# Talking-heads attention and a Fourier mixing layer on one core: two halves of a softmax step parted, memory laid out anew, and a join between two phases reordered

## The chip, the core and the metric

The kernel runs on one core of one Trainium2 chip. The metric is the time of the whole kernel in device microseconds (us). Three runs before the change took 2463.07, 2463.15 and 2467.11 us; the median is 2463.15 us. The profiled run took 2461.87 us and its recorded span is 2460.1 us, at a mean granted TensorE clock of 0.989 of full speed.

The engines are named as the profile names them: PE (matrix products), PEld (loading of weights into PE), DVE (vector engine), ACT (scalar engine), POOL (GpSimd) and SP (the engine that here only issues transfers). [...]

## What is computed

The batch is 8, there are 12 heads, 448 positions and 64 values per head. All is float32; the layer's weights arrive as float64 and are converted on the chip.

```python
# attention, "talking heads": heads are mixed before and after the softmax
scores = scale * np.matmul(q, k.transpose(0, 1, 3, 2))      # (8, 12, 448, 448)
scores = np.einsum('bhij,hg->bgij', scores, w_pre)          # first mixing
scores = scores - np.max(scores, axis=-1, keepdims=True)
attn = np.exp(scores)
attn = attn / (np.sum(attn, axis=-1, keepdims=True) + 1e-09)
attn = np.einsum('bhij,hg->bgij', attn, w_post)             # second mixing
x = np.matmul(attn, v)          # then (8, 12, 448, 64) -> (8, 448, 768)
# Fourier mixing and a feed-forward layer
mixed = np.real(np.fft.fft(np.fft.fft(x, axis=1), axis=2))
u = x + mixed
un = (u - mean(u)) / np.sqrt(var(u) + 1e-06)                # by row
out = u + np.maximum(un @ w_ch1, 0.0) @ w_ch2               # 768 -> 3072 -> 768
```

## The kernel before

There are two phases. The first (attention and Fourier transform) goes in 192 steps; a step takes ten rows of scores of all twelve heads through both mixings and the softmax. The second (feed-forward) takes 42 pairs of blocks of matrix products; it is a Strassen-like scheme with seven products in place of eight.

The order of the engines' work in a step is fixed by hand. Step `s` holds the first mixing of step `s + 2` (LM is 2), the second mixing of step `s`, and pieces of other work (`take`) that are dealt out over the steps: scores (QK), the product with v (AV), and "full" pieces, which are transposes of q, k and X and the Fourier products.

```python
    with tc.manual_schedule(engines={ET.PE, ET.DVE, ET.Activation, ET.Pool}):
        while s <= TOT - GS + AT_X[-1]:
            old = len(later)
            n = take("none", s)                 # loads
            if 0 <= s + LM < TOT:
                emit_premix(s + LM)             # PE: first mixing
            flush()
            if 0 <= s < TOT:
                emit_postmix(s)                 # PE: second mixing
            if 0 <= s + LM < TOT:
                emit_max(s + LM)                # DVE: two maxima
                emit_exp(s + LM)                # ACT: two exponentials
            take("AV", s)
            if 0 <= s < TOT:
                emit_turn(s)                    # DVE: transpose of the second mixing
            if s >= 4:
                wts.deal(1)                     # DVE: one operation on the weights
            take("QK", s)
            ...                                 # SP: gather for step s + 4
            if 0 <= s + LM < TOT:
                emit_scale(s + LM)              # DVE: reciprocal; POOL: scaling
            ...
            for _ in range(min(len(folds), 1 if n and s > 3 else 2)):
                folds.pop(0)()                  # POOL: sums for the Fourier transform
            take("full", s)
            s += 1
        flush()
        while folds:
            folds.pop(0)()
        wts.deal(1000)
```

The first mixing and its softmax. `mx` is one tile of two PSUM banks (512 float32 each), and its pool holds one of them; `nmx` is one tile for both halves. The four products of the first mixing use four quarters of the PE array (64 rows by 64 columns each).

```python
    pmx = pool("pmx", space=bass.MemoryType.PSUM)          # one buffer
    ...
    def emit_premix(T):
        mx = pmx.tile([P, 2, 512], F32, name="mx", tag="mx")
        Kr = steps[T]["Kr"]
        for x in range(2):
            for z in range(2):
                nc.tensor.matmul(mx[64 * z:64 * z + 64, x, :S],
                                 kw1[64 * x:64 * x + KR, :],
                                 Kr[64 * x:64 * x + KR, z, :], start=True, stop=True)

    def emit_max(T):
        nmx = psm.tile([P, 2], F32, name="nmx", tag="nmx")
        for x in range(2):
            nc.vector.tensor_reduce(nmx[:, x:x + 1], steps[T]["mx"][:, x, :S],
                                    axis=AX.X, op=ALU.max, negate=True)

    def emit_exp(T):
        ...
        for x in range(2):
            nc.scalar.activation(PP[:, x, :], steps[T]["mx"][:, x, :S], ACTF.Exp,
                                 bias=steps[T]["nmx"][:, x:x + 1],
                                 accum_out=den[:, x:x + 1])
```

Waits are set by tile: an instruction that reads a tile waits for all that was written to it, and the next user of a buffer waits until all readers of the last one are done. The gather of a step's scores (`Kr<-Sb`) is four transfers from SP. The tables of the Fourier transform are loaded by POOL in step 3, though they are first used in step 38 (`AT_Z`):

```python
    def emit_tables():
        for t, n in ((rows, "at"), (ts, "ts"), (tcs, "tc")):
            for p, m in _split(0, t.shape[0]):
                nc.gpsimd.dma_start(out=t[p:p + m], in_=cn[n].ap()[p:p + m])
    ...
    due("none", 3, emit_tables)
```

The join of the phases. The second phase needs the mean and the variance of the first 512 rows (`stats`), a power of the variance on POOL (`power`), the normalised rows from ACT (`norm`), their transposes (`turn`) and sums of them (`total`). Its pools are opened after those of the first phase are closed, so they lie on the same memory, and their first use waits for the last use of what lay there.

```python
    for t in range(2):
        load_u(t)
    for i in ORDER:
        load_w1(0, i)
    with tc.manual_schedule(engines={mybir.EngineType.PE, mybir.EngineType.DVE}):
        for x in range(NT2):
            stats(0, x)          # DVE
        power(0)                 # POOL, four small operations
        for x in range(NT2):
            norm(0, x)           # ACT
            turn(0, x)           # PE, ACT
        for n in range(4):
            total(0, n)          # DVE
        ...
        for n in range(NC * NTB):
            ...
            second(n, first(n))
```

## Time and profile before

| what | value |
|---|---|
| median of three runs | 2463.15 us |
| span of the profiled run | 2460.1 us |
| PE busy | 2373.4 us (96%) |
| DVE busy | 1518.6 us (62%) |
| ACT busy | 787.0 us (32%) |
| POOL busy | 779.9 us (32%) |
| moved by DMA | 372.09 MB, 151 GB/s on average |

Busy time is the union of an engine's recorded instructions. Matrix products are pipelined and their ends are modelled, so a busy PE can hide a short wait between two of them. A row of the profile's fifth part, or of a timeline, gives line, engine, operation, the tiles (`out<-in`), the shape and the count. In square brackets, or after the bar, stands how long the engine was idle before it, and what ended that idle time. L470 is the first mixing, L478 the maximum, L486 the exponential, L507 the second mixing, L444 the scores, L534 the product with v, L941 and L997 the products of the second phase. The profile cuts the span into 40 slices:

```
PE   6999999999999969999999999999999999999999
DVE  3678778788877636776566455654575467533333
ACT  3666666666666533232011011111101101111110
POOL 3577877768775541121111001100110011000000
PEclk8999999999999989999999999999999999999999
```

A slice is 61.5 us. The first phase fills slices 1 to 14, and the 6 at place 15 is the join.

### The profile page before, as it was taken

The numbers are of one execution on the slowest core, as the hardware profiler recorded it, in microseconds if no ns is written. First come the engines' busy times: TensorE is split into PE (matmuls) and PEld (weight loads), VectorE is DVE, ScalarE is ACT, GpSimd is POOL, SyncE is SP. The second block draws the span as 40 slices with busy tenths as digits, with TensorE's granted clock in tenths as the row PEclk, the third lists the DMA queues.
The fourth block names the chain that finished last, engine by engine and source line by source line (L and its number), as shares of the span: only waits on it lengthen the run. The fifth ranks groups of instructions, "written<-read, shape, count | busy, mean of one in ns | idle before, by whom it ended". The sixth has DMA issues, their size and how long they took to land.

```text
span 2460.1 us, 48351 instructions
## 1 busy us (share of the span) xinstructions
PE 2373.4 (96%) x18608; PEld 1536.8 (62%) x18608; DVE 1518.6 (62%) x3103; ACT 787.0 (32%) x2059; POOL 779.9 (32%) x1292
## 2 busy tenths in 40 slices
PE   6999999999999969999999999999999999999999
PEld 2344454444444457777777777777777777777776
DVE  3678778788877636776566455654575467533333
ACT  3666666666666533232011011111101101111110
POOL 3577877768775541121111001100110011000000
PEclk8999999999999989999999999999999999999999
DMA  5554555546554464635545354436444545343331
GB/s 137 163 168 157 173 167 170 178 150 192 169 167 141 148 220 139 190 119 203 178 144 159 102 190 135 148 102 197 131 141 130 184 123 157 120 155 118 120 116 52
DMA packets 168579, 372.09 MB, mean 151 GB/s; under 512 B 36734, under 2 KB 90006, under 8 KB 168350
## 3 DMA queue, kind: packets, MB, share of 16 engines
q1 hardware_dynamic: 129038, 260.22, 32.4%
q0 software_dynamic: 33744, 107.40, 15.0%
q8 instruction: 148, 2.42, 0.4%
q10 hardware_dynamic: 5568, 1.38, 0.3%
q14 instruction: 81, 0.66, 0.1%
HBM read 211.98 MB, written 74.34 MB: 116 GB/s over the span
## 4 chain that ended last, share of the span: by engine, by line
PE 84%; DVE 5%; ACT 4%; DMA 3%; POOL 2%; issue 1%; SPq 1%; ACTq 0%; POOLq 0%; DVEq 0%
PE psP L941 18%; PE psP L997 18%; PE psR L941 9%; PE psR L997 9%; PE mx L470 6%; PE ms L534 5%; PE psQ L997 4%; PE psQ L941 4%; PE po L507 4%; ACT PP L486 3%; PE ms L444 3%; DVE nmx L478 3%; DMA Kr<-Sb 2%; PE ms L648 2%; PE ms L632 1%
## 5 line engine op out<-in xcount | busy, mean ns | idle before, releaser
L941 PE MATMUL psP<-ub,w1t 128*128 128x256 f32 x2016 | 463.9, 380 | 0.0
L997 PE MATMUL psP<-w2t,h 128*128 128x384 f32 x1344 | 460.9, 486 | 0.0
L941 PEld LDWEIGHTS psP<-ub,w1t 128*128 128x128 f32 x2016 | 384.0, 191 | 61.1
L207 POOL DMA_DIRECT2D raw<-in_moe_w_ch_dram x120 | 68.8, 574 | 918.6 <-DVE tmp L251 905.6
L997 PEld LDWEIGHTS psP<-w2t,h 128*128 128x128 f32 x1344 | 254.4, 190 | 165.9
L486 ACT ACTIVATE PP<-mx,nmx 128x448 f32<-128x448 f32 x384 | 239.9, 629 | 275.5 <-DVE nmx L478 258.3
L497 POOL TENSOR_SCALAR PP<-PP,rcp 128x448 f32<-128x448 f32 x384 | 241.2, 637 | 261.7 <-DVE rcp L495 208.7
L478 DVE TENSOR_REDUCE nmx<-mx 128x1 f32<-128x448 f32 x384 | 221.2, 618 | 127.1 <-PE mx L470 116.9
L1003 DVE TENSOR_TENSOR u<-u,psP 128x384 f32<-128x384 f32 x336 | 183.3, 552 | 141.5 <-PE psP L997 139.3
L946 ACT COPY h<-psP 128x512 f32<-128x512 f32 x42 | 24.6, 585 | 765.7 <-PE psP L941 745.7
L470 PE MATMUL mx<-Kr,kw 60*64 60x448 f32 x1536 | 204.3, 560 | 43.5 <-ACT PP L486 33.8
L941 PE MATMUL psR<-ub,w1t 128*128 128x256 f32 x1008 | 231.3, 379 | 0.0
L997 PE MATMUL psR<-w2t,h 128*128 128x384 f32 x672 | 230.5, 486 | 0.0
L952 DVE TENSOR_TENSOR h<-h,psQ 128x512 f32<-128x512 f32 x42 | 28.9, 687 | 302.1 <-PE psQ L941 302.1
L518 DVE STREAM_TRANSPOSE Pv<-po 128x896 f32<-128x896 f32 x192 | 212.3, 1106 | 2.9 <-PE po L507 2.6
L941 PEld LDWEIGHTS psR<-ub,w1t 128*128 128x128 f32 x1008 | 191.4, 190 | 25.9
L507 PE MATMUL po<-PP,kw 60*32 60x448 f32 x3072 | 190.0, 552 | 0.8 <-DVE Pv L518 0.8
L444 PE MATMUL ms<-kT,qT 64*60 64x448 f32 (+1 forms) x1536 | 188.3, 555 | 0.0
L324 ACT COPY Sb<-ms 124x448 f32<-124x448 f32 x384 | 184.7, 541 | 8.1 <-DMA Kr<-Sb 3.8
L534 PEld LDWEIGHTS ms<-Pv,vv 64*64 64x64 f32 x5376 | 141.9, 132 | 71.0 <-issue 30.9
L997 PEld LDWEIGHTS psR<-w2t,h 128*128 128x128 f32 x672 | 127.2, 190 | 87.5
L534 PE MATMUL ms<-Pv,vv 64*64 64x120 f32 x5376 | 164.3, 267 | 2.1 <-issue 2.1
(92 smaller groups left out, 2738.4 us busy)
## 6 DMA issues: line engine op xcount, KB each, us to landing
ub<-ub SPq DMA_DIRECT2D x294, 384.0 KB
Kr<-Sb SPq DMA_DIRECT2D x768, 105.0 KB
raw<-in_moe_w_ch_dram POOLq DMA_DIRECT2D x72, 256.0 KB, 3.4
raw<-in_moe_w_ch_dram POOLq DMA_DIRECT2D x48, 384.0 KB, 3.8
w<-wst POOLq DMA_DIRECT2D x126, 128.0 KB, 3.1
w<-wst POOLq DMA_DIRECT2D x84, 192.0 KB, 3.2
w1t<-w SPq DMA_DIRECT2D x42, 384.0 KB
w2t<-w SPq DMA_DIRECT2D x42, 384.0 KB
```

What stands on the lines that cost most here:

```text
L324: (nc.scalar.copy if eng == "a" else nc.vector.tensor_copy)(out=out, in_=in_)
L444: nc.tensor.matmul(pss[x][64 * y:64 * y + r0 + 64 - lo, :S], st["qT", xx][64 * x:64 * x + 64, y, lo:r0 + 64], st["kT", xx][64 * x:64 * x + ...
L470: nc.tensor.matmul(mx[64 * z:64 * z + 64, x, :S], kw1[64 * x:64 * x + KR, :], Kr[64 * x:64 * x + KR, z, :], start=True, stop=True)
L478: nc.vector.tensor_reduce(nmx[:, x:x + 1], steps[T]["mx"][:, x, :S], axis=AX.X, op=ALU.max, negate=True)
L486: nc.scalar.activation(PP[:, x, :], steps[T]["mx"][:, x, :S], ACTF.Exp, bias=steps[T]["nmx"][:, x:x + 1], accum_out=den[:, x:x + 1])
L497: nc.gpsimd.tensor_scalar(PP[:, x, :], PP[:, x, :], rcp[:, x:x + 1], 1.0, op0=ALU.mult, op1=ALU.mult)
L507: nc.tensor.matmul(po[o:o + 32, z, :S], kw2[64 * z:64 * z + KR, y, :], PP[64 * z:64 * z + KR, :, c * HS:(c + 1) * HS], start=True, stop=True)
L518: nc.vector.transpose(g["Pv"][:, T % GT, :].rearrange("p (z s) -> p z s", z=2), steps[T]["po"][:, :, :S])
L534: nc.tensor.matmul(pss[y][64 * x:64 * x + 64, :nu * R], st["v", pr][64 * y:64 * y + 64, x, jb * D:(jb + 1) * D], _ap(Pv, 64 * y * rp + 32 ...
L941: nc.tensor.matmul(p[:, m, :], w1[i][:, kc, m * P:(m + 1) * P], ub[:, kc, :], start=i in OPENS and m == kc == 0, stop=kc == NK - 1, skip_g ...
L997: nc.tensor.matmul(p, lhs[i][:, kf, x * P:(x + 1) * P], w2[i][:, kf, :], start=i in OPENS and kf == 0, stop=kf == FM - 1, skip_group_check ...
L1003: nc.vector.tensor_tensor(us_, us_, p, op=ALU.add)
```

## The change

Four things are changed.

1. The first mixing's PSUM tile becomes two tiles of one bank, and the maxima become two tiles of one column. Thus the exponential of the first half depends only on the first half's maximum, and the next step's first half of the mixing only on the first half's exponential. Instructions and their order on each engine stay.
2. The pools of both phases are ordered by when their content is last used, so that the second phase's first tiles lie on memory that is free early.
3. The last folds (sums on POOL that the Fourier transform of the last batch needs) are taken out of the end of the first phase and stand behind the power of the first rows, which POOL's fixed order now includes.
4. The tables are loaded in four parts, in steps 9, 16, 17 and 19.

```diff
     psb = pool("psb", 2)
     pkr = pool("pkr", 3)
-    pvv = pool("pvv")
     ppp = pool("ppp", 3)
     psm = pool("psm", 4)
+    cst = pool("cst")
+    wts.open(ctx, tc)
+    pvv = pool("pvv")
     ppv = pool("ppv", 2)
 ...
-    wts.open(ctx, tc)
-    cst = pool("cst")
 ...
-    def emit_tables():
-        for t, n in ((rows, "at"), (ts, "ts"), (tcs, "tc")):
-            for p, m in _split(0, t.shape[0]):
-                nc.gpsimd.dma_start(out=t[p:p + m], in_=cn[n].ap()[p:p + m])
+    def emit_table(t, n, p0, p1):
+        for p, m in _split(p0, p1 - p0):
+            nc.gpsimd.dma_start(out=t[p:p + m], in_=cn[n].ap()[p:p + m])
 ...
     def emit_premix(T):
-        mx = pmx.tile([P, 2, 512], F32, name="mx", tag="mx")
+        mx = [pmx.tile([P, 512], F32, name="mx", tag=f"mx{x}") for x in range(2)]
         for x in range(2):
             for z in range(2):
-                nc.tensor.matmul(mx[64 * z:64 * z + 64, x, :S],
+                nc.tensor.matmul(mx[x][64 * z:64 * z + 64, :S],
 ...
     def emit_max(T):
-        nmx = psm.tile([P, 2], F32, name="nmx", tag="nmx")
+        nmx = [psm.tile([P, 1], F32, name="nmx", tag=f"nmx{x}") for x in range(2)]
         for x in range(2):
-            nc.vector.tensor_reduce(nmx[:, x:x + 1], steps[T]["mx"][:, x, :S],
+            nc.vector.tensor_reduce(nmx[x][:, :], steps[T]["mx"][x][:, :S],
 ...
-            nc.scalar.activation(PP[:, x, :], steps[T]["mx"][:, x, :S], ACTF.Exp,
-                                 bias=steps[T]["nmx"][:, x:x + 1],
+            nc.scalar.activation(PP[:, x, :], steps[T]["mx"][x][:, :S], ACTF.Exp,
+                                 bias=steps[T]["nmx"][x][:, :],
 ...
-    due("none", 3, emit_tables)
+    for at, t in ((9, (rows, "at", 0, PN)), (16, (ts, "ts", 0, PN)),
+                  (17, (tcs, "tc", 0, CW // 2)), (19, (tcs, "tc", CW // 2, CW))):
+        due("none", at, lambda t=t: emit_table(*t))
 ...
         flush()
+        wts.deal(1000)
+
+    def fold_rest():
         while folds:
             folds.pop(0)()
-        wts.deal(1000)
 ...
 # second phase
+    pst = pool("pst", 4)
+    pun = pool("pun", 2)
     pu = [pool("pu")]
+    pub = pool("pub", 11)
     pw1 = pool("pw1", 7)
-    pub = pool("pub", 11)
-    pun = pool("pun", 2)
     pw2 = pool("pw2", 7)
     ph = pool("ph")
-    pst = pool("pst", 4)
 ...
-    with tc.manual_schedule(engines={mybir.EngineType.PE, mybir.EngineType.DVE}):
+    ET = mybir.EngineType
+    with tc.manual_schedule(engines={ET.PE, ET.DVE, ET.Pool}):
         for x in range(NT2):
             stats(0, x)
         power(0)
+        fold_rest()
+    with tc.manual_schedule(engines={ET.PE, ET.DVE}):
         for x in range(NT2):
             norm(0, x)
```

In the program that results, the order of PE's, DVE's and ACT's instructions in the steps is unchanged. At the join it moves: the statistics of the first 512 rows stand among DVE's last work of the first phase; on POOL the power stands ahead of the last group's twelve sums; on ACT the first two `norm` stand ahead of the first phase's last copies (sixteen of XT, four of X), and on PE three transposes of the second phase stand after the second of the six transposes of the second-last X.

## The prediction

> **What bounds the kernel now.** I read the busy shares by window first, then the waits, then two timelines and the chain of waits. The first view cuts the span at the first mixing's first and last step (31.20 and 859.95 us) and at the first product of the second phase (903.14 us). Columns: window, its length, each engine's busy us (instructions), granted clock, DMA share, GB/s.

> ```profile
> 31.20:859.95 828.75, 786.24 (x11994) 368.57 (x11995) 637.36 (x1254) 539.04 (x1627) 581.35 (x932) 0.99 0.53 165
> 859.95:903.14 43.19, 22.69 (x437) 17.07 (x437) 13.28 (x29) 14.73 (x45) 27.65 (x42) 0.76 0.71 236
> 903.14:2460.10 1556.96, 1549.89 (x6097) 1142.18 (x6096) 861.09 (x1802) 223.42 (x372) 165.50 (x299) 1.00 0.45 142
> ```

> The second phase, 1557 us, has PE busy 99.5% and the diff leaves it alone. What can be won lies ahead of it: PE idles 828.75 - 786.24 = 42.5 us in the steps and 43.19 - 22.69 = 20.5 us at the join, 63 us in all, or 2.6% of the whole. A gain over 2% (49 us) would need nearly all of it.

> The steps come in two kinds. In the timeline of an early one the engines hand over to each other, and no two of them overlap:

> ```profile
> 47.63 0.98 PE L470 MATMUL mx<-Kr,kw 60*64 60x448 f32 x8 [0.96 <-ACT PP L486]
> 48.76 1.16 DVE L478 TENSOR_REDUCE nmx<-mx 128x1 f32<-128x448 f32 x2 [0.78 <-PE mx L470]
> 50.03 0.63 ACT L486 ACTIVATE PP<-mx,nmx 128x448 f32<-128x448 f32 x1 [1.60 <-DVE nmx L478]
> 50.66 0.62 ACT L486 ACTIVATE PP<-mx,nmx 128x448 f32<-128x448 f32 x1
> 51.43 0.98 PE L470 MATMUL mx<-Kr,kw 60*64 60x448 f32 x8 [0.99 <-ACT PP L486]
> ```

> From one first mixing to the next: 1.13 to the maxima, 1.16 for both, 0.11, 0.63 for one exponential, 0.77 from the second's start to the release. That is 3.80 us, and PE has only three groups of 0.91 (first mixing, second mixing, scores), 2.73 us, in it. In a later step the product with v is there too, and PE has no gap (here 417.71 is a v product, then scores, then the next first mixing):

> ```profile
> 416.80 0.98 PE L507 MATMUL po<-PP,kw 60*32 60x448 f32 x16
> 417.71 1.71 PE L534 MATMUL ms<-Pv,vv 64*64 64x120 f32 x56
> 419.20 0.97 PE L444 MATMUL ms<-kT,qT 64*64 64x448 f32 x8
> 419.95 0.97 PE L470 MATMUL mx<-Kr,kw 60*64 60x448 f32 x8
> ```

> Start to start that is 0.91 + 0.91 + 1.49 + 0.75 = 4.06 us. So PE sets a step with a v product, and the chain of mixing, maximum and exponential sets a lean one.

> The chain of waits shows the tables' collision, and the join:

> ```profile
> 66.06 10.96 DMA Kr<-Sb
> ...
> 890.20 3.79 POOL xf L609 x4
> 893.99 1.02 POOL mv L893
> 895.01 0.07 issue
> 895.08 0.20 POOL mv L894
> ...
> 895.65 1.03 ACT un L903
> ```

> A gather of step 8's scores is issued at 66.06 and lands at 77.02, just after the tables were issued (57.67 to 60.9). At the join the power (mv) comes behind 3.79 us of sums on POOL, though its input was ready at 884.5, and ACT and PE wait for it, PE for 16.9 us.

> [...] Here twelve products took 4.14 us after the idle stretch (903.14) and 2.75 us at 911.02.

> **Part 1, the halves.** Nothing is added or removed; waits get finer. The first exponential can start one maximum earlier (0.54), and the next first half of the mixing waits for the first exponential only. A half's own loop becomes 1.13 + 0.62 + 0.11 + 0.77 = 2.63 us in place of 3.80. So a lean step falls to what comes next: PE's 2.73 plus some lost overlap, as the halves of the mixing start 0.63 apart instead of together, or DVE's queue: 1.16 maxima, 1.10 transpose, 0.37 reciprocal, about 0.4 for a weights operation, 3.05. I take 3.15.

> I sorted the 191 step intervals by what PE has between two first mixings, and set each against the PE spacing of its pieces (0.91, 0.91, scores 0.90, v 1.45, six transposes 0.85, seven 0.98, z pair 1.56, second Fourier product 1.26):
> - scores only, 19 steps, median 3.81 against 2.72. Of these, four hold other waits (first step, tables, gathers). The other 15 average 3.9: 15 x 0.75 = 11, and the four give 2.
> - scores and six transposes, 17 steps, 8.4 us over PE's spacing in all: the chain's 0.2 each, and a few where DVE came late. Those also get the chain's new 1.17 us of slack. I take 5.
> - scores and v, 82 steps, median 4.09 against 4.09; 13.5 over in all, but 6.6 of it are gathers in steps 8 and 24. Of the 6.9 left, half: 3.5.
> - the rest, 16 us over in all; many at PE's wall: 5.

> Sum 26.5. Some will run into DVE, or into gathers that are wanted sooner; I keep three quarters: 20 us.

> **Part 2, tables.** Steps 7, 8 and 9 took 3.98, 8.85 and 5.08 where like ones take 3.79, 4.09 and 3.79: 6.2 us. Later batches load v at the same place without tables and have no such step. Steps 16 to 19 have no loads of q, k or v. [...] I keep 4.5 us.

> **Part 3, the join.** The program's order decides. On POOL the power now stands behind the second-last fold, which ended at 876.5, and ahead of the last: 0.25 + 1.05 + 0.20 + 0.24 = 1.75, so it ends at 878.2 in place of 895.6. That is 17 us earlier, but I don't count 17: ACT's two norms now stand ahead of copies that PE's last v products need (those were at 869.5). PE therefore stops at about 869.9 and goes on when a norm is done, 879.3. Step by step from there: ACT's second norm to 880.3, four XT copies to 881.1, PE's last four transposes of the second-last X 0.7, the last v products 7.0 (870.68 to 877.70 before), the second Fourier product 1.56, the last X 0.85: PE is through at about 891. Then the other 21 transposes, paced by ACT: two X copies 0.9, eight ub copies of 0.48 less the first, two norms of 1.03, about 6. The first product starts at about 897 rather than 903.14: 6 us. PE is warm by then, which gives back the 4.14 - 2.75 = 1.4 of the first twelve products[...]. The last fold (12.4 us of POOL) starts after the last X copy at about 892 and ends at 904; its first reader came 13 us after the first product, so at 910: no new wait. I take 7.

> **Part 4, memory.** The statistics waited until 877.8 for memory that the v products had used. They now run among DVE's last steps, some 10 us earlier; that is what makes the early power possible and is counted there.

> Sum: 20 + 4.5 + 7 = 31.5, 2463.15 - 31.5 = 2431.6 us.

> **Rivals.** (a) PE is the wall nearly everywhere, and the chain's slack is eaten by DVE (637 of 829 us busy, with bursts): then only the lean steps give, 8 us, and the sum is 8 + 4.5 + 7: 2444. For it: the waits of the first mixing on the exponential are only 27.3 us on PE in 60 to 860 us. Against: DVE idles 190 us in the steps. (b) The halves of the mixing run apart and lose their overlap: eight instructions of 0.54 to 0.56 pass in 0.98 because four quarters work at once. If half of all steps lost 0.4, 40 us would be given back and the kernel would be slower, 2470. Against: where PE is the wall both exponentials are over before PE comes to the mixing (419.63 against 419.95), so the halves still start together. (c) The join turns against itself: the early norms hold ACT while DVE's early statistics wait for rows that SP now issues after the last gather, and the last reciprocals stand behind them. Then part 3 gives nothing or costs a few us: 2440. (d) The join is better than I think, as the statistics and the power overtake the fold and the 9 us pause is not there: 8 more, 2423.

> **Range and chances.** Parts 1 and 3 carry the doubt: 10 to 33 for the first, 0 to 15 for the third, 2 to 6 for the tables. Their sum lies between 16 and 47 with some 8 in 10, so 2416 to 2447. Over 2% faster (below 2413.9) needs nearly everything: 0.08. Slower by 2% has only (b), and more than it: 0.01. The rest is 0.91.

> **What would show it.** In the changed profile: the lean steps' spacing at about 3.1 in place of 3.79; the v steps still at 4.06 to 4.1; no first exponential behind both maxima; PE's idle time between the first and last first mixing at about 20 us in place of 42.5; step 8 at some 4.1; the power's end near 878 less the earlier gains (about 25), followed by the norm at once; PE stopped for about 9 us ahead of it. I am wrong if the lean steps stay at 3.8 (another chain holds them), if v steps fall below 4.0 (then PE wasn't their wall), or if the second phase's 1557 us change.

## The result, and the profile after

| kernel | median us (runs) | ratio to before, 95% interval |
|---|---|---|
| before, beside it | 2463.11 (4) | |
| changed | 2425.35 (4) | 0.9847 [0.9826, 0.9868] |

The change gains 37.8 us, or 1.5%. The profile after is of a run of 2431.02 us, the slowest of the four, so it shows somewhat less than the median does. First the busy shares by window of the changed kernel, cut at the same three events as before: the first mixing's first step, its last step, and the first product of the second phase. Columns: window, length, busy us of PE, PEld, DVE, ACT and POOL (instructions), granted clock, DMA share, GB/s.

```profile
31.14:838.33 807.19, 795.46 (x11995) 382.52 (x11995) 629.31 (x1255) 552.85 (x1627) 580.86 (x934) 1.00 0.54 168
838.33:873.89 35.56, 22.27 (x437) 16.98 (x437) 12.41 (x28) 14.17 (x45) 19.80 (x31) 0.86 0.65 210
873.89:2429.20 1555.31, 1548.51 (x6098) 1141.17 (x6096) 863.94 (x1802) 223.75 (x372) 176.07 (x309) 1.00 0.45 145
```

Against the profile before, the steps lost 21.6 us, the join 7.6, the second phase 1.65. These are single executions: three kernels below whose steps work as before the change (part 3 with and without the layout, and the maxima parted alone) took 835.0 to 835.7 us for the steps, where the profile before has 828.75, so a gain in the steps is known to some 7 us only. PE's idle time in the steps (length less busy time) fell from 42.5 to 11.7 us. It did not fall by 21.6 but by more: PE's busy time rose by 9.2 us with the same instructions, since a first mixing whose halves start apart counts as busy while its quarters follow each other (all first mixings: 204.3 us busy before, 223.9 after).

A lean step of the changed kernel in its timeline (start, duration, engine, line, and in brackets the idle time and what ended it). L469 is the first mixing, L477 the maximum, L485 the exponential:

```profile
352.31 0.99 PE L469 MATMUL mx<-Kr,kw 60*64 60x448 f32 x8
353.37 1.16 DVE L477 TENSOR_REDUCE nmx<-mx 128x1 f32<-128x448 f32 x2 [1.38 <-PE mx L469]
354.09 0.63 ACT L485 ACTIVATE PP<-mx,nmx 128x448 f32<-128x448 f32 x1 [0.51 <-DVE nmx L477]
354.71 0.63 ACT L485 ACTIVATE PP<-mx,nmx 128x448 f32<-128x448 f32 x1
354.95 2.03 PE L469 MATMUL mx<-Kr,kw 60*64 60x448 f32 x7
```

The first exponential (354.09) begins while the second maximum still runs (353.37 + 1.16 = 354.53), and the next mixing comes 2.64 us after the last one; the same step took 3.81 before. PE writes that mixing's first half (from 354.95) while ACT still reads the second half of the last one (354.71 + 0.63 = 355.34). The last line also shows the price: this mixing takes 2.40 us (2.03 for the seven products that the view holds) instead of 0.98, since its quarters now start when their own half, and their own gather, is ready.

The waits of the changed kernel between 31 and 860 us show what ended PE's idle time (sum in us, times, longest):

```profile
PEld mx L469 <- DMA Kr<-Sb: 25.7, 32, 3.3
PEld mx L469 <- ACT PP L485: 18.9, 40, 1.4
PE mx L469 <- DMA Kr<-Sb: 9.7, 10, 2.5
```

Before, in the same window, the exponential stood first with 94.8 us on PEld and 33.8 on PE, and the gather had 15.5 and 7.4. The chain is nearly gone from PE's own waits (0.9 us behind the exponential), and the gather has become the first of them. (PEld's waits are not time lost as they stand: before, they came to 94.8 us behind the exponential alone, while PE idled 42.5 us in all the steps.)

Last, the join of the changed kernel in its timeline. L897 and L900 are the first and last operation of the power, L908 the norm, L917 the transpose for the second phase, L566 the transposes of X:

```profile
855.43 0.25 POOL L897 TENSOR_SCALAR mv<-mv 128x4 f32<-128x4 f32 x1
857.19 0.24 POOL L900 TENSOR_SCALAR mv<-mv 128x4 f32<-128x4 f32 x1
857.47 1.94 ACT L908 ACTIVATE un<-u,mv 128x768 f32<-128x768 f32 x2 [10.63 <-POOL mv L900]
858.55 0.90 PE L917 MATMUL psQ<-ident,un 128*128 128x128 f32 x3 [9.55 <-ACT un L908]
859.80 1.20 PE L566 MATMUL ms<-ident,XT 128*113 128x128 f32 x4 [0.35 <-ACT XT L324]
873.89 2.75 PE L946 MATMUL psP<-ub,w1t 128*128 128x256 f32 x12
```

The statistics were done at 847.9, but POOL was at the second-last group's sums until 855.3. ACT and PE wait for the power, PE for 9.55 us where it waited 16.9 before, and the last four transposes of the second-last X (859.80) follow behind. ACT keeps the program's order here: the v products whose copies these transposes need ended at 848.58, ACT stood still for 10.63 us, and the copies (L324, from 859.32) came only after both norms.

### The profile page after: what moved, and what is told of

It reads as the page before. It is cut to its first block, busy times and chain, and to the rows that moved or that the text cites. A ratio compares the mean times of both kernels' runs of the same rounds, so it can differ in the third digit from the quotient of the medians.

```text
span 2429.2 us, 48510 instructions
## 1 busy us (share of the span) xinstructions
PE 2381.3 (98%) x18608; PEld 1550.1 (64%) x18608; DVE 1512.6 (62%) x3103; ACT 800.5 (33%) x2059; POOL 782.1 (32%) x1293
## 3 DMA queue, kind: packets, MB, share of 16 engines
q10 hardware_dynamic: 5568, 1.38, 0.4%
## 4 chain that ended last, share of the span: by engine, by line
PE 93%; DMA 3%; SPq 1%; DVE 1%; ACT 1%; issue 0%; ACTq 0%; DVEq 0%
PE psP L946 18%; PE psP L1002 18%; PE psR L946 9%; PE psR L1002 9%; PE mx L469 7%; PE po L506 6%; PE ms L443 6%; PE ms L533 6%; PE psQ L1002 5%; PE psQ L946 4%; DMA Kr<-Sb 2%; PE ms L647 2%; PE ms L420 1%; PE ms L631 1%; SPq L459 1%; PE ms L566 1%
## 5 line engine op out<-in xcount | busy, mean ns | idle before, releaser
L477 DVE TENSOR_REDUCE nmx<-mx 128x1 f32<-128x448 f32 x384 | 222.7, 618 | 130.8 <-PE mx L469 128.2
L485 ACT ACTIVATE PP<-mx,nmx 128x448 f32<-128x448 f32 x384 | 240.5, 631 | 172.4 <-DVE nmx L477 160.3
L469 PE MATMUL mx<-Kr,kw 60*64 60x448 f32 x1536 | 223.9, 551 | 11.0 <-DMA Kr<-Sb 9.7
L324 ACT COPY Sb<-ms 124x448 f32<-124x448 f32 x384 | 184.8, 540 | 20.5 <-DMA Kr<-Sb 8.8
L443 PE MATMUL ms<-kT,qT 64*64 64x448 f32 (+1 forms) x1536 | 189.1, 554 | 0.0
```

Source lines behind the costliest of these rows:

```text
L324: (nc.scalar.copy if eng == "a" else nc.vector.tensor_copy)(out=out, in_=in_)
L443: nc.tensor.matmul(pss[x][64 * y:64 * y + r0 + 64 - lo, :S], st["qT", xx][64 * x:64 * x + 64, y, lo:r0 + 64], st["kT", xx][64 * x:64 * x + ...
L469: nc.tensor.matmul(mx[x][64 * z:64 * z + 64, :S], kw1[64 * x:64 * x + KR, :], Kr[64 * x:64 * x + KR, z, :], start=True, stop=True)
L477: nc.vector.tensor_reduce(nmx[x][:, :], steps[T]["mx"][x][:, :S], axis=AX.X, op=ALU.max, negate=True)
L485: nc.scalar.activation(PP[:, x, :], steps[T]["mx"][x][:, :S], ACTF.Exp, bias=steps[T]["nmx"][x][:, :], accum_out=den[:, x:x + 1])
```

## The experiments

Each kernel was run on the same chip as the kernel before, whose median there was 2465.9 to 2467.6 us. Where no medians are named, a gain in us is the ratio's share of that median; the difference of the bare medians is up to 1.5 us larger. "Steps" and "join" are the first two windows above; in the profile before they took 828.75 and 43.19 us.

### Each part alone

**Part 1 alone.** The kernel before, with this edit (and what reads these tiles changed to match):

```diff
-        mx = pmx.tile([P, 2, 512], F32, name="mx", tag="mx")
+        mx = [pmx.tile([P, 512], F32, name="mx", tag=f"mx{x}") for x in range(2)]
-        nmx = psm.tile([P, 2], F32, name="nmx", tag="nmx")
+        nmx = [psm.tile([P, 1], F32, name="nmx", tag=f"nmx{x}") for x in range(2)]
```

> The kernel before with the two halves of the first mixing's PSUM tile and of the maxima as tiles of their own, nothing else. Theory (the halves carry most of the gain): 18 to 24 us faster than before, 2439 to 2445; lean steps at about 3.1 to 3.3 us in place of 3.79; steps 7 to 9 still hold the stall beside the table loads. Rival (PE is the wall nearly everywhere, and the tables or the join carry the gain): 8 us or less, 2455. The join, from the last first mixing to the first product of the second phase, stays at 43 us under both.

Measured: 2436.94 us, 0.9878 [0.9857, 0.99], some 30 us. In its profile the steps take 808.37 us (20.4 less than in the profile before, 27 less than the 835 of the other kernels with the old steps), PE idles 10.7 us in them, and step 8, with the tables still where they were, takes 10.06 us. The join is 40.12 us, 3.1 shorter although nothing there was edited. PE's long pause is still there:

```profile
873.11 3.02 PE L912 MATMUL psQ<-ident,un 128*128 128x128 f32 x12 [16.88 <-ACT un L903]
```

So the halves carry about four fifths of the change. Of the join's 3.1 us, 2.13 are an idle stretch of PE ahead of a v product (876.60 before) that this kernel doesn't have. It is no chance of one profile: with the mixing's tile parted alone (below) it is missing too and the join is 40.22 us, and with the maxima parted alone it is there and the join is 43.17. What makes it wasn't found.

**Part 3 with the layout.** The kernel before, with the new order of pools and with

```diff
-        while folds:
-            folds.pop(0)()
         wts.deal(1000)
+    def fold_rest():
+        while folds:
+            folds.pop(0)()
 ...
-    with tc.manual_schedule(engines={mybir.EngineType.PE, mybir.EngineType.DVE}):
+    with tc.manual_schedule(engines={ET.PE, ET.DVE, ET.Pool}):
         ...
         power(0)
+        fold_rest()
```

> The kernel before with the new memory layout and the fold behind the power, without halves and tables. Theory: the join falls from 43 to about 35.5 us and the second phase starts warm, together 9 us faster, 2454; PE stops for about 9.5 us in the join, until the first norm. Rival (the join only shifts a wait, or the early statistics hold the last steps): 0 to 3 us, 2460 to 2463.

Measured: 2458.58 us, 0.9968 [0.9959, 0.9978], about 7.9 us. The join takes 36.15 us, and PE's pause is 10.6 us:

```profile
886.66 0.77 PE L567 MATMUL ms<-ident,XT 128*113 128x128 f32 x2 [10.60 <-ACT XT L324]
```

The line says what PE waits for: a copy of XT, which is the first phase's own work and stands behind the norms on ACT.

**Part 2 alone.** The kernel before, with

```diff
-    due("none", 3, emit_tables)
+    for at, t in ((9, (rows, "at", 0, PN)), (16, (ts, "ts", 0, PN)),
+                  (17, (tcs, "tc", 0, CW // 2)), (19, (tcs, "tc", CW // 2, CW))):
+        due("none", at, lambda t=t: emit_table(*t))
```

> The kernel before with the tables in four parts in steps 9, 16, 17 and 19, nothing else. Theory of the prediction: steps 7 to 9 lose 6 us of stall, 4.5 us faster in all, 2458.6. Rival (the stall of step 8 comes from the loads of v and of the next batch that stay where they are; the changed kernel still took 7.08 us for step 8): 0 to 2 us, 2461 to 2463.

Measured: 2462.88 us, 0.998 [0.9971, 0.9989], about 4.9 us. Steps 7, 8 and 9 took 3.79, 4.10 and 3.76 us, where they took 3.98, 8.85 and 5.08 before; in the five other kernels with the tables in their old place step 8 took 9.06 to 10.14 us. The v loads, which stayed in their place, are not the cause. The profile as a whole doesn't show the 4.9 us: its steps took 826.76 us, 2.0 less than in the profile before, and its join, which wasn't edited, 46.04, 2.9 more (PE stood still for 2.96 us where it stood for 2.13).

**The fold order without the layout.** As the part 3 kernel, but with all pools in their old order.

> The kernel before with the last fold behind the power, but with the old memory layout. Theory A (only the order on POOL matters): the statistics still end at 884.5, the power follows at once and ends at about 886.5, PE doesn't stop among the last v products, and the first product of the second phase starts about 9 us earlier: 2454 or a little less, as good as with the layout. Theory B (the layout is what makes the power early): 0 to 3 us, 2460 to 2463.

Measured: 2456.67 us, 0.9961 [0.9948, 0.9974], about 9.6 us; the join takes 34.06 us. Its timeline:

```profile
884.61 0.10 POOL L854 MEMSET mhalf<- 128x4 f32 x1 [1.69 <-PE ms L534]
891.39 0.25 POOL L896 TENSOR_SCALAR mv<-mv 128x4 f32<-128x4 f32 x1 [3.09 <-DVE mv L892]
894.52 3.01 PE L916 MATMUL psQ<-ident,un 128*128 128x128 f32 x12 [7.89 <-ACT un L907]
```

POOL's first write to the second phase's memory waits for the v products, the statistics come later, and the power ends 27.1 us after the last first mixing (893.41 and 866.30), where it ended 19.3 us after it with the layout (884.43 and 865.16). And yet the join is 2.1 us shorter, in one profile of each. A late norm finds the first phase's copies already done, so PE stops for a norm once and then makes twelve transposes in a row; an early norm stands ahead of the copies that PE needs (with the layout, v products ended at 876.06, and ACT copied them from 885.40 only, behind a norm). The layout isn't needed for the gain.

**The changed kernel again**, unedited, beside three of the kernels that follow (without the layout, with the second-last fold held back, and with a quarter of the gather issued by ACT):

> The changed kernel once more, as the base for the three kernels that run beside it on the same chip. Both theories: 0.985 of the kernel before, about 38 us faster.

Measured: 2427.45 us, 0.9844 [0.983, 0.9859]. In its profile the steps took 802.24 us, 5 less than in the first profile of the same kernel, and the join 34.89.

**The whole change without the layout**, that is parts 1, 2 and 3 on the old pools:

> The changed kernel with the old memory layout: halves, tables and fold order alone. Theory A (the layout isn't needed once the power stands ahead of the fold, since with it ACT and PE wait for the power among the last v products): equal to the changed kernel or up to 2 us faster. Theory B (the layout gives the loads and the statistics their early start): 5 us or more slower than the changed kernel.

Measured: 2423.92 us, 0.983 [0.9816, 0.9845]: not slower than the change, and the intervals overlap. The join takes 31.32 us against 34.89 in the repeat of the change. Its timeline shows the power's last operation and the end of PE's pause:

```profile
854.73 0.25 POOL L900 TENSOR_SCALAR mv<-mv 128x4 f32<-128x4 f32 x1
856.10 3.02 PE L917 MATMUL psQ<-ident,un 128*128 128x128 f32 x12 [6.79 <-ACT un L908]
```

The power ends 24.4 us after the last first mixing (854.98 and 830.63), 5 us later than with the layout, and the pause is shorter.

### Which of the two parted tiles

Part 1 parts two things: the mixing's tile and the maxima. These two kernels are part 1 with one of them left whole.

**The mixing's tile parted, the maxima one tile:**

```diff
-        nmx = [psm.tile([P, 1], F32, name="nmx", tag=f"nmx{x}") for x in range(2)]
+        nmx = psm.tile([P, 2], F32, name="nmx", tag="nmx")
```

> The kernel before with only the PSUM tile of the first mixing parted; the maxima stay in one tile, so both exponentials wait for both maxima. Chain of a half: 1.13 + 1.16 + 0.11 + 0.77 = 3.17 us in place of 3.80. Theory (any cut that brings the chain under the other limits of a step, PE's spacing and SP's 3.26 us, gives most of the gain): 20 us or more of the 30 us that both parts gave. Rival (the slack of both parts is needed): half of it, 12 to 15 us.

**The maxima parted, the mixing's tile whole:**

```diff
-        mx = [pmx.tile([P, 512], F32, name="mx", tag=f"mx{x}") for x in range(2)]
+        mx = pmx.tile([P, 2, 512], F32, name="mx", tag="mx")
```

> The kernel before with only the maxima parted; the mixing's PSUM stays one tile, so the next first mixing waits for both exponentials, as before, but the first exponential starts one maximum earlier. Chain: 3.80 - 0.54 = 3.26 us. Theory: 20 us or more of the 30 us, and the first mixing keeps its four products together (0.98 us), which the parted PSUM tile loses where the exponentials come late. Rival: half of it, 12 to 15 us.

Measured: 2442.69 us, 0.9911 [0.989, 0.9931], for the first; 2466.33 us, 0.9997 [0.9989, 1.0005], for the second. What was expected of the second fell. Of the first the gain came, 22 us, but not by the chain that was expected: its exponential doesn't wait for both maxima. In its timeline it starts 0.71 us after the maxima begin:

```profile
154.77 1.16 DVE L478 TENSOR_REDUCE nmx<-mx 128x1 f32<-128x448 f32 x2 [1.36 <-PE mx L470]
155.48 0.63 ACT L486 ACTIVATE PP<-mx,nmx 128x448 f32<-128x448 f32 x1 [0.51 <-DVE nmx L478]
```

In that of the second it starts 1.27 us after them, behind both, as it did before the change:

```profile
51.30 1.16 DVE L478 TENSOR_REDUCE nmx<-mx 128x1 f32<-128x448 f32 x2 [0.78 <-PE mx L470]
52.57 0.63 ACT L486 ACTIVATE PP<-mx,nmx 128x448 f32<-128x448 f32 x1 [1.60 <-DVE nmx L478]
```

The waits of the two built programs say the same. These are two exponentials of one step on ACT, first of the kernel with the mixing's tile whole, then of the one with it parted:

```
Activation PP,den<-mx,nmx 128x448 [waits DVE, PE, Pool]
Activation PP,den<-mx,nmx 128x448

Activation PP,den<-mx,nmx 128x448 [waits DVE, Pool]
Activation PP,den<-mx,nmx 128x448 [waits DVE]
```

The waits for DVE are these in all 192 steps. With one tile of two banks there is a single wait for DVE, ahead of both exponentials, and it falls behind the second maximum. It cannot be for the maxima, which are two tiles there; it is ACT's reading of the mixing's tile that is put behind DVE's reading of it. Why one reading is put behind the other isn't shown: no run tried them without this order. With a tile for each half it is gone between the halves: each exponential waits for its own maximum, and the first begins 0.71 us after the maxima where it began 1.27 us after them. PE's waits change with it: with one tile the next first mixing waits once, for the second exponential, and with the tile parted each half waits for its own. These two savings come together, and no run parts them. The maxima's column of SBUF is told apart without being a tile of its own. So what was said of the kernel before, that an instruction which reads a tile waits for all that was written to it, does not hold for the maxima.

Parting the maxima adds no wait and takes none away: the built program of the first kernel has the same instructions as part 1 whole, in the same order and with the same waits on every engine, and that of the second has those of the kernel before. The profiles of the first kernel and of part 1 whole agree to 0.6 us in the span (2434.0 and 2434.5) and 0.2 in the steps. Their medians, 2442.69 and 2436.94, are 5.75 us apart all the same (runs of the first reach from 2435.8 to 2455.48), which shows how far two measurements of one and the same order of work can lie apart here.

### What remains after the change

**The second-last fold behind the power too.** The change, with

```diff
-            for _ in range(min(len(folds), 1 if n and s > 3 else 2)):
+            for _ in range(min(len(folds), 1 if n and s > 3 else 2) if s < TOT - 3 else 0):
```

> The changed kernel, with the second-last fold also held back until the power is done, so that POOL comes to the power about 9 us earlier. Theory (PE's 9.55 us pause in the join is the fold ahead of the power, and nothing else waits behind it): the pause falls to about 2 us, the join from 35.6 to about 28 us, the kernel 7 us faster than the changed one. Rival (the folds, now 21 us in one piece behind the power, come too late for the Fourier products of the second phase, or PE only waits for the next thing): 0 to 2 us.

Measured: 2421.2 us, 0.9815 [0.9801, 0.9829], 6.3 us less by the medians than the change beside it, and just clear of its interval. The join takes 29.55 us. Its timeline:

```profile
850.83 0.25 POOL L897 TENSOR_SCALAR mv<-mv 128x4 f32<-128x4 f32 x1 [2.84 <-DVE mv L893]
852.88 1.95 ACT L908 ACTIVATE un<-u,mv 128x768 f32<-128x768 f32 x2 [3.71 <-POOL mv L900]
853.96 0.55 PE L917 MATMUL psQ<-ident,un 128*128 128x128 f32 x3 [3.48 <-ACT un L908]
```

POOL now waits for the statistics, not they for POOL. The pause is 3.48 us instead of 9.55: 6.1 us less, and the join is 6.0 us shorter than in the first profile of the change, 5.3 than in its repeat. The pause was on the path, and the second-last fold made most of it.

**A quarter of the gather issued by ACT.** The chain of waits of the changed kernel still goes through gathers early on:

```profile
43.66 5.14 DMA Kr<-Sb
...
58.29 6.95 DMA Kr<-Sb
```

SP needs 3.2 us to issue one step's four transfers (0.81 us from one to the next), and lean steps now come every 2.6 us. The edit:

```diff
-                nc.sync.dma_start(
+                (nc.scalar if x and z else nc.sync).dma_start(
```

> The changed kernel with one of the four transfers of each step's gather issued by ACT in place of SP. Theory (with the halves parted, the next wall of the lean steps is SP, which issues four transfers of 0.81 us, 3.26 us a step): lean steps go below 3.0 us, the waits of the first mixing on its gather fall from 35 us to under 25, and the kernel gets 3 to 8 us faster than the changed one. Rival (the transfers' landing or ACT itself is the wall, since ACT now issues as well): no gain, or up to 10 us slower.

Measured: 2422.62 us, 0.983 [0.9815, 0.9845], against 0.9844 [0.983, 0.9859] for the change beside it: the medians are 4.8 us apart, as the theory said, but the intervals overlap. The first mixing waited 25.0 us for gathers (PE and PEld), against 24.4 in the repeat of the change and 35.4 in its first profile, and steps 1 to 7 took 25.11 us, against 26.04. That SP's issuing holds the gathers is not supported; whether there is a gain isn't decided.

**Both of these edits:**

> The changed kernel with both finds: the second-last fold behind the power as well, and one of four transfers of each gather issued by ACT. Theory (the two lie in different stages and add up): 0.980 of the kernel before, 10 to 11 us faster than the changed one. Rival (ACT's earlier gathers and the join's loads collide): no better than the better of the two alone, 0.9815.

Measured: 2419.21 us, 0.9805 [0.9791, 0.9818]. Clear of the change, not clear of the kernel with only the fold held back.

**Gathers one step earlier.** The last kernel, with scores, the transposes ahead of them, and gathers all a step earlier:

```diff
-AT_T = ((12, 10), (17, 16), (14, 18))
+AT_T = ((11, 9), (16, 15), (13, 17))
-    LG, LM = 4, 2
+    LG, LM = 5, 2
-                due("QK", f + BS * n - 7 + AT_QK[n][xx],
+                due("QK", f + BS * n - 8 + AT_QK[n][xx],
```

> The last kernel (folds held, ACT issues one transfer of four) with scores, their transposes and the gathers one step earlier: five steps ahead of the second mixing in place of four. Theory (what still holds lean steps is the time from copied scores to the mixing: 3.3 us of issue and 3 to 7 us of landing must fit in the lead): the waits of the first mixing on its gather fall from 23 to 27 us to under 15, the opening steps 1 to 7 from 26 to about 22 us, the kernel to 0.977 or 0.978 of the one before, 5 to 8 us faster than without the longer lead. Rival ([...] the gather waits for its buffer, of which there are still three): the same 0.9805.

Measured: 2417.52 us, 0.9798 [0.9784, 0.9811], the lowest of all and not to be told from the last. The first mixing's wait for gathers fell from 22.6 to 6.1 us, as expected, and yet the steps did not get shorter in the profile (802.90 us, against 796.05), and steps 1 to 7, expected at about 22 us, took 27.79, against 24.93. The waits of this kernel, between 31 and 860 us:

```profile
PEld mx L469 <- ACT PP L485: 44.1, 83, 3.5
...
ACT Sb L324 <- DMA Kr<-Sb: 15.3, 20, 4.9
...
PEld mx L469 <- DMA Kr<-Sb: 4.6, 13, 1.1
```

In the kernel without the lead these three are 23.2, 7.8 and 17.7 us. The wait moved rather than went: the copies of scores into `Sb` now wait until the gathers of that buffer's last content are done (it has two buffers), ACT stands still there, and the exponentials are behind those copies in its queue. That the one wait makes the other is read from this order and not shown by a run; a third `Sb` buffer wasn't tried.

## Why the prediction was right or wrong

**The time.** 2431.6 us was predicted, 2425.35 came; the gain of 31.5 us was 37.8. The result lies in the range, and within 2%, as given most weight. The first profile of the change is 30.9 us shorter than the one before, the repeat's 37.4. In the repeat's the steps gave 26.5 us, where 24.5 were kept for parts 1 and 2, and the join and the second phase 9.9, where 7 were.

**Part 1: the mechanism right, its terms mis-sized both ways, and one cause wrongly named.** Twenty us were kept; the part alone gave some 30. Of these, 3.1 lie in the join and 1.4 in the second phase, where none were counted for it; in the steps it is 20.4 us against the profile before and about 27 against the other kernels with the old steps. The first mis-sized term is the lean step, taken as 3.15 us. It measured 2.57 to 2.63 where nothing else waits (steps 30, 33, 78, 102, 174, 180, 182; 3.75 to 4.35 before). The 3.15 leaned on DVE's 3.05, a sum of durations. In the timeline of step 78 DVE's instructions start at 353.37 (maxima), 354.44 (transpose), 355.47 (weights), 355.71 and 355.90 (reciprocal) and 355.99 (next maximum): 2.62 us for the round, since one starts before the record of the last ends (353.37 + 1.16 = 354.53). PE's three groups in the same step are spaced 0.92, 0.91 and 0.81, 2.64. So PE, DVE and the half's own loop all stand at 2.6, and there was no lost overlap to add. PE's idle time in the steps, expected at about 20 us, came to 11.7 (8.1 in the repeat).

By what PE has in them, the steps of the two profiles of the changed kernel compare so:

| steps with | count | before, us | after | after, again | term of the sum |
|---|---|---|---|---|---|
| first and second mixing, at most scores | 21 | 90.8 | 68.9 | 69.4 | 13, tables apart |
| scores twice | 7 | 26.5 | 23.7 | 23.7 | in the next |
| transposes | 40 | 157.1 | 148.5 | 149.5 | 5 |
| v | 83 | 353.3 | 351.0 | 351.3 | 3.5 |
| Fourier products | 40 | 200.9 | 215.1 | 208.4 | in "the rest", 5 |

My classes were cut a little differently, but the pattern is plain: the lean steps and those with transposes gave more than I counted, those with v kept their 4.09 (medians 4.08 and 4.10), as predicted, and the Fourier steps didn't give 5 but took 7.5 to 14 back. That the steps came out near the 20 us is thus partly luck: too little was counted for the lean steps and too much for these. (The row of v is not firm: in the five profiles with the old steps it lies between 353 and 361 us, while that of the Fourier products keeps within 200 and 202. And the pieces that the prediction lists for a step with v, 0.91, 0.91, 0.90 and 1.45, sum to 4.17, not to the 4.09 that it sets against them.) Two kinds of Fourier steps that grew are seen. The Fourier step right after a lean one (steps 55, 79, 103, 127, 151, 175) grew by 5.2 us in all (4.8 in the repeat): in step 79 the mixing's last quarters waited 0.72 us for a gather that used to be there in time. And steps 136 and 160 were 2.5 and 5.0 us longer in one profile, 1.4 and 0.8 in the other. In the first profile a copy into `Sb` in step 136 waited 3.57 us for the gathers of that buffer's last content, with PE behind it; in step 160 PE waited 2.49 us for a gather, and then its clock stood at half from 710.4 to 713.8. This is the "gathers that are wanted sooner" for which a quarter was taken off; it is also most of why these two profiles of one kernel differ by 5 us in the steps (6.7 us in the Fourier steps).

The change's text, and the prediction's "the first exponential can start one maximum earlier", put that to the parted maxima as much as to the parted mixing tile. Only the mixing tile does it: 0.9997 with the maxima alone.

**Part 2: right.** 4.5 us was kept of 6.2, which was my estimate; 4.9 was measured, and steps 7 to 9 alone came back to their like. In the whole change step 8 still took 7.08 us (5.21 in the repeat), now without tables beside it: most likely since faster steps ask for its gather sooner. The product of the three parts' ratios is 0.9878 x 0.9968 x 0.998 = 0.9827, the whole is 0.9847 (0.9844 in the repeat). Given the intervals these don't contradict each other, so a loss between the parts is possible and not shown.

**Part 3: right, nearly to the term.** 7 us was taken, 7.9 measured with the layout. Predicted and measured: the power's end 18.3 and 19.1 us after the last first mixing; PE's pause 9.4 and 9.55; the first product 37 and 35.6 after that mixing; 1.4 and 1.65 us in the second phase, with PE's clock at full when it starts, as was said, though part 1 alone has that too with the long pause left in place (last section).

**Part 4: wrong.** The layout was said to be "what makes the early power possible". The power does come 5 to 8 us earlier with it, but in this order of POOL's work that gains nothing: without it the join is 2.1 and 3.6 us shorter in the profiles, and the times are as good. The early norms block ACT for the copies of the first phase (10.63 us in the changed kernel), which the prediction saw (the pause), but not that this cancels the layout's use here. It isn't shown to be useless: with the second-last fold held back the power waits for the statistics, which the layout makes early, and that join, 29.55 us, is shorter than the 31.32 of the change without the layout. The held-back fold on the old layout wasn't tried.

**The rivals.** (a), PE and DVE as the wall and 8 us for part 1, fell with the part alone. (b), halves that run apart, is there in kind: first mixings longer than 1.2 us rose from 17 to 44 of 192, and all first mixings together keep PE busy for 19.6 us longer than before. But PE's idle time fell by 30.8 us, so most of this fills time that was idle. (c), a join that turns against itself, shows in small: 1.53 us of PE behind a late reciprocal, 0.70 of a statistic waiting for rows. (d), a join without the pause, named 8 us that were to be had, but not by this change: the second-last fold stood in its way, and holding it back gave 6.

The two kernels with the fold held back and ACT issuing a quarter of the gathers beat both the kernel before and the change: 2419.21 and, a step earlier, 2417.52 us.

## What to carry to other kernels

Part a PSUM tile where two engines read its halves one after the other (the mixing's tile, parted alone, gave 22 us); look in the built waits for a reader that waits for another reader, and whether an edit changes any wait: parting the maxima changed none. When a chain goes, compare durations start to start, not by their sum, to see which engine is the next wall, and expect the transfers to be asked for sooner. An earlier result helps only if what it releases doesn't stand ahead of more urgent work on an engine that keeps the program's order, as the norms did for 10.63 us on ACT: order that work before moving the memory.

## What the runs showed of the hardware that was not expected

The second phase's first twelve products took 2.75 us in the changed kernel and 4.14 before. The prediction puts that to PE being "warm" or not after the idle stretch. PE's granted clock it is, but the length of the pause doesn't set it. The traces record when the granted clock stood at half:

| kernel | longest pause of PE in the join, us | last stretch at half clock, us | the products start at | they took, us |
|---|---|---|---|---|
| before | 16.88 | 882.1 to 905.9 | 903.14 | 4.14 |
| maxima parted alone | 16.89 | 888.1 to 912.0 | 909.04 | 4.23 |
| part 1 alone | 16.88 | 859.8 to 876.9 | 878.95 | 2.75 |
| changed | 9.55 | 853.7 to 864.0 | 873.89 | 2.75 |
| second-last fold held back | 3.48 | 868.4 to 871.9 | 870.00 | 3.67 |
| gathers a step earlier | 1.96 | 861.4 to 864.8 | 862.19 | 4.06 |

In each row the time is 2.75 us and half of what the products still have of the stretch, to 0.03 us: before, 905.9 - 903.14 = 2.76, and 2.75 + 1.38 = 4.13.

PE did not have to stand still for the clock to fall to half: in the last row the window ahead of the stretch (858.0 to 861.4) had 1.77 us of recorded work in it and no pause over 0.76 us.
